# Sigmoid attention and two gated MLPs in float32 parts: GpSimd's share of the weight and operand splitting goes to VectorE and ScalarE, with a new order of loads, identity products ahead of the scores, and other places for some steps

## The chip, the cores and the metric

The kernel runs on one core of a Trainium2 chip. The metric is the device time of one execution in microseconds (us). A core has five engines that run side by side and wait for one another by semaphores: TensorE (PE: products into PSUM), VectorE (DVE), ScalarE (ACT), GpSimd (POOL), and SyncE (SP), which here only issues DMAs. Each engine works off its own list in order.

## The reference

Four batches of 448 rows. Attention has 12 heads of 64, with a sigmoid in place of the softmax; its output, 448 x 768 for each batch, goes through two gated MLPs one after the other, the second with a residual.

```
scores = q k^T / sqrt(64) - log(448);  attn = sigmoid(scores);  x = attn v
MLP 1: h = relu(x w_in);  u, v = halves of h (512 each)
       vn = (v - mean) / sqrt(var + 1e-6)
       x' = (u * (w_spatial vn + b_spatial)) w_out
MLP 2: the same with gelu, vn * g_ln, its own weights, and x' = x + (...) w_out
```

Inputs and weights of the MLPs come as 64-bit floats where the reference has them so (w_in, w_out); the kernel turns them into 32-bit ones itself.

## The kernel before

**Products in parts.** A 32-bit number is split into a high part in a short format (`fp32r`) and the low rest, `lo = x - hi`. A product of two such operands is three products (high x high, high x low, low x high). High parts are written by ScalarE (a cast), low parts by a subtraction.

**Attention** (lines 274 to 445) runs in 12 groups of 4 heads, n = 0 to 11, three to a batch, and each group in 4 rounds, r = 0 to 3, of 128 rows of k (the last has 64). Round s = 4n + r does on TensorE `scores(n, r)` (L357, 24 products of 32 rows side by side into two PSUM tiles `sc`, of which there are three) and `values` of the round two before (L381, into `av`). ScalarE makes the sigmoid of both `sc` tiles (L368). Behind that each round has a step of preparation for the next group: at r = 0 `turn(n+1)` (VectorE transposes k and q, L312 to L317), at r = 1 `high(n+1)` (L325 by VectorE, L328 by ScalarE), at r = 2 `low(n+1)`: two subtractions, that of k by VectorE and that of q by GpSimd (L337). At r = 1 `gather(n-1)` copies the finished `av` of the last group to `x` (L395, VectorE), and only then the next `values` of r = 0 may write there. Loads: `load_qk(n+2)` at r = 1, `load_v(n+2)` at r = 2 (eight small DMAs), `load_v(1)` in round 0.

**The belt.** Weights of the first MLP are made ready meanwhile. `convert` (L152) is a generator for one piece of 128 x 256 64-bit numbers; each `yield` ends what it does in one tick. It loads the piece (L158), squares the upper words (`g`), makes the 32-bit number from the two words by three integer steps on VectorE (L169, L173, L177), sets tiny ones to zero with `g` (L183), casts the high part (L191) and subtracts for the low part (L193). With `early` (27 pieces during attention) GpSimd squares (L164) and subtracts (L193); later ScalarE squares and VectorE subtracts. `belt.tick(new)` lets each running job do one step and starts `new` jobs; in attention it is called once a round, with a new piece in each of rounds 0 to 7 and then in each odd one. `load_w_sp` (spatial weights, four jobs) runs on the belt `spatial` in the last rounds.

**The MLPs** (from L651) take the batches in turn. For each: `hv` (v half, four row blocks, L474), `hu` (u half, L519), `sp` (spatial product, L538, then L544 or L546, L550, and the split of the gated `u` into `gh` by ScalarE, L551, and `gl` by VectorE, L555), `wo` (L572). Between them `fill` ticks three belts; `chain` holds the low-part steps, `gl` among them. `fill(..., waits=True)` ticks `chain` behind the conversions. `store_last` (L605) transposes the last batch by products with `ident` and writes it out by three pairs of DMAs.

Of the kernel before, what the change touches and what calls it, by code (L numbers as in the profile page):

```python
# [9 lines left out]
F32 = mybir.dt.float32  # L10
# [4 lines left out]
ALU = mybir.AluOpType  # L15
# [5 lines left out]
def raw(ap):  # L21
    return ap.bitcast(F32)
# [3 lines left out]
def tile_sigmoid_attention_two_gated_mlps(  # L26
# [125 lines left out]
    def convert(src, n, part, at, keep, early=False):  # L152

        w = stg.tile([P, PIECE, 2], I32, tag="w", name="w", bufs=4)
        dst = w.rearrange("p (c f) two -> p c (f two)", c=n)
        nc.sync.dma_start(out=dst if n > 1 else dst[:, 0], in_=src)  # L158
        yield
        f = stg.tile([P, PIECE], I32, tag="f", name="f", bufs=4)  # L160
        g = stg.tile([P, PIECE], F32, tag="g", name="g", bufs=2)
        low, high = w[:, :, 0], w[:, :, 1]
        if early:
            nc.gpsimd.tensor_tensor(  # L164
                out=g, in0=high.bitcast(F32), in1=high.bitcast(F32), op=ALU.mult
            )
        else:
            nc.scalar.activation(g, high.bitcast(F32), AF.Square)  # L168
        nc.vector.tensor_scalar(  # L169
            out=f, in0=high, scalar1=3, scalar2=0x3FFFFFF8, op0=ALU.logical_shift_left,  # L170
            op1=ALU.bitwise_and,
        )
        nc.vector.scalar_tensor_tensor(  # L173
            out=f.bitcast(U32), in0=low.bitcast(U32), scalar=29, in1=f.bitcast(U32),
            op0=ALU.logical_shift_right, op1=ALU.bitwise_or,
        )
        nc.vector.scalar_tensor_tensor(  # L177
            out=f, in0=high, scalar=-0x40000000, in1=f, op0=ALU.bitwise_and, op1=ALU.bitwise_or
        )
        if early:  # L180
            yield
        f = f.bitcast(F32)
        nc.vector.scalar_tensor_tensor(  # L183
            out=f, in0=g, scalar=TINY * TINY, in1=f, op0=ALU.is_ge, op1=ALU.mult
        )
        yield
        if keep is not None:
            nc.sync.dma_start(out=keep[:, at:at + PIECE], in_=f)
            return
        hi, lo = part()  # L190
        nc.scalar.copy(out=hi, in_=f)  # L191
        yield
        (nc.gpsimd if early else nc.vector).tensor_tensor(  # L193
            out=lo, in0=f, in1=raw(hi), op=ALU.subtract
        )

    def refetch(part, at, n, keep):

# [75 lines left out]
    def attention(apool, epool, ps_att, done):  # L274
# [55 lines left out]
        def low(n):  # L330
# [7 lines left out]

            if n > 0:
                part(nc.vector, 1, slice(0, S))  # L340
                part(nc.gpsimd, 3, slice(0, S))
            else:
                part(nc.vector, 1, slice(0, P))
                part(nc.vector, 3, slice(0, S))
                part(nc.vector, 1, slice(P, S))
# [64 lines left out]
        load_qk(0)  # L410
        load_qk(1)
        load_v(0)
        turn(0)
        high(0)
        low(0)
        for s in range(4 * NG + 2):
# [9 lines left out]
            if n + 1 < NG:  # L426
# [3 lines left out]
                    high(n + 1)  # L430
                elif r == 2:
                    low(n + 1)
            if n + 2 < NG:
                if r == 1:
                    load_qk(n + 2)
                elif r == 2:
                    load_v(n + 2)
            if s == 0:
                load_v(1)
            elif s == 4 * NG - 9:  # L440
                load_vecs(l1)
            belt.tick(1 if s < 8 else s % 2)
            if s >= 4 * NG - 6:
                spatial.tick(1)
        return lambda: gather(NG - 1)

# [1 line left out]
    class Mlp:  # L448
# [111 lines left out]
        def wo(self, b, i, after=None):  # L560
# [8 lines left out]
            for m in range(KD):  # L569
# [7 lines left out]
                for c in done if i == KF - 1 else ():  # L577
                    x = xs[b // 2][:, c, (b % 2) * S:(b % 2 + 1) * S]
                    if L.n == 1:
                        nc.scalar.copy(out=x, in_=self.o[c][:, :S])  # L580
                    else:
                        nc.vector.tensor_tensor(out=x, in0=self.o[c][:, :S], in1=x, op=ALU.add)
                if after and m > 1:
                    after(m - 2)
            if after:
                after(KD - 2)
                after(KD - 1)

    def store(pool, b, m):

# [13 lines left out]

    def store_last(o, pr, m):  # L605

        t = bank()
        for j in range(3, 7):
            nc.tensor.transpose(
# [2 lines left out]
        dst, src = o[:, :, m * P:(m + 1) * P], t.rearrange("p (j f) -> p j f", j=4)  # L612
        if m == KD - 2:
            nc.vector.tensor_copy(out=dst, in_=src)
        else:
            nc.scalar.copy(out=dst, in_=src)
        if m % 2:
            ms = slice((m - 1) * P, (m + 1) * P)
            eng = nc.scalar if m == KD - 1 else nc.sync
            nc.sync.dma_start(  # L620
                out=out[2 * pr + 1, :3 * P, ms].rearrange("(j p) m -> p j m", p=P), in_=o[:, 1:, ms]
            )
            eng.dma_start(out=out[2 * pr + 1, 3 * P:, ms], in_=o[REST:, 0, ms])

    with tc.manual_schedule():
        make_identity(nc, ident)
# [22 lines left out]
        with tc.tile_pool(name="fpool", bufs=1) as fpool:  # L649
# [9 lines left out]
            for n, (m, b) in enumerate(seq):  # L659
# [3 lines left out]
                def fill(new=0, more=(), waits=False):  # L663


                    if refill:
                        belt.waiting += more
                    if not waits:
                        chain.tick()
                    spatial.tick(1)  # L670
                    belt.tick(new)
                    if waits:
                        chain.tick()

                def split_next(c):
                    if nxt:
# [40 lines left out]
                m.sp(b, 1)  # L717
                fill(0 + refill, waits=True)
                m.wo(b, 0)
                fill(1, w_o(0))  # L720
                split_next(2)
                m.sp(b, 2)
                if refill:
                    spatial.waiting = [load_w_sp(l2, j) for j in range(4)]
                fill(0 + refill, waits=True)
                m.wo(b, 1)
                fill(1, w_o(1))
                split_next(4)
                m.sp(b, 3)
                fill(1, waits=True)  # L730
                m.wo(b, 2)
                fill(0 + refill, w_o(2))
                if refill:
# [44 lines left out]
```

## Time and profile before

| | us |
|---|---|
| median of 3 runs | 597.42 (596.37 to 600.14) |
| the profiled execution, its own time | 597.48 |
| its span, first to last instruction | 595.7 |
| busy in the span: TensorE, VectorE, ScalarE, GpSimd | 571.4, 410.0, 251.6, 98.9 |

All times in the trace count from the span's start; 1.8 us of the execution lie outside it. A row of the timeline has start, length, engine, line, operation, tiles and count, and in brackets how long the engine idled before it and what ended that. Lengths of TensorE's rows overlap, since products are pipelined.

### The profile page before, as it was taken

To read this page: it belongs to the slowest core of one execution; us is meant where nothing else is said; L and a number is where in the kernel's file an instruction comes from. 1 tells how busy PE (TensorE), PEld (TensorE's weight loads), DVE (VectorE), ACT (ScalarE), POOL (GpSimd) and SP (SyncE) were. 2 spreads that over 40 slices of the span, in tenths; PEclk is the share of its full clock that TensorE was granted. 3 is DMA by queue.
4 is the path that set the end of the run, shared out by engine and by line. 5 is a ranking of instruction groups with operands and counts; after the bars stand their busy time and mean duration, and the time that the engine had idled before them with its cause. 6 is when DMAs were issued, how large, how long until landed. Compare 5 with 4: busy or idle time off the path is not lost.

```text
span 595.7 us, 9520 instructions
## 1 busy us (share of the span) xinstructions
PE 571.4 (96%) x3568; PEld 456.5 (77%) x3568; DVE 410.0 (69%) x805; ACT 251.6 (42%) x418; POOL 98.9 (17%) x127
## 2 busy tenths in 40 slices
PE   4969999999999999999999999999999999999996
PEld 2535555555469888998888899888989988998995
DVE  4599999999976985894688357669444545544433
ACT  4647877787724434433423345534221313212112
POOL 0445465445221001000200100020010002001000
PEclk9979999999999999999999999999999999999999
DMA  6854446545311212532242224520004100500502
GB/s 185 226 182 136 139 145 196 166 138 119 62 60 35 72 53 72 159 107 62 87 153 80 80 73 114 123 54 18 1 1 77 17 0 12 83 1 0 82 13 92
DMA packets 85405, 51.74 MB, mean 87 GB/s; under 512 B 56112, under 2 KB 75376, under 8 KB 85360
## 3 DMA queue, kind: packets, MB, share of 16 engines
q1 hardware_dynamic: 85280, 51.08, 31.7%
q8 instruction: 28, 0.46, 0.3%
q14 instruction: 17, 0.14, 0.1%
q10 hardware_dynamic: 80, 0.07, 0.0%
HBM read 41.68 MB, written 9.44 MB: 86 GB/s over the span
## 4 chain that ended last, share of the span: by engine, by line
PE 73%; DVE 13%; DMA 4%; issue 3%; ACT 3%; POOL 2%; SPq 1%; DVEq 0%; ACTq 0%
PE t L519 13%; PE t L474 12%; PE sc L572 12%; PE av L381 10%; PE sc L357 10%; PE t L538 10%; PE av L572 6%; DMA w<-in_moe_w_in_dram 2%; DVE f L177 2%; DVE f L173 1%; DMA inq<-in_q_dram 1%; DVE st L483 1%; DVE f L183 1%; POOL st L488 1%; DVE vr L493 1%
## 5 line engine op out<-in xcount | busy, mean ns | idle before, releaser
L368 ACT ACTIVATE a<-sc,small 128x896 f32<-128x896 f32 (+1 forms) x96 | 92.8, 1006 | 32.6 <-PE sc L357 32.3
L357 PEld LDWEIGHTS sc<-ops 32*128 32x128 f32 x1152 | 57.5, 194 | 46.5 <-ACT a L368 25.2
L357 PE MATMUL sc<-ops 32*128 32x448 f32 x1152 | 80.0, 397 | 9.0 <-ACT ops L328 7.5
L519 PE MATMUL t<-xh,uh 128*128 128x448 f32 x192 | 69.9, 364 | 0.9 <-ACT u L523 0.9
L485 POOL TENSOR_SCALAR st<-st 128x1 f32<-128x1 f32 x28 | 10.6, 378 | 356.7 <-DVE st L484 356.7
L381 PE MATMUL av<-a,vt 128*64 128x448 f32 x288 | 64.7, 572 | 5.2 <-DVE x L395 5.0
L519 PE MATMUL t<-xh,ul 128*128 128x448 f32 x192 | 69.5, 362 | 0.0
L519 PE MATMUL t<-xl,uh 128*128 128x448 f32 x192 | 69.3, 361 | 0.0
L474 PE MATMUL t<-vh,xl 128*128 128x512 f32 x168 | 65.7, 391 | 1.3 <-DVE xl L463 1.2
L538 PE MATMUL t<-sh,v 128*128 128x448 f32 x224 | 65.9, 363 | 0.6 <-DVE gt L544 0.6
L474 PE MATMUL t<-vh,xh 128*128 128x512 f32 x168 | 65.6, 390 | 0.0
L474 PE MATMUL t<-vl,xh 128*128 128x512 f32 x168 | 65.4, 389 | 0.0
L551 ACT CAST gh<-u 128x448 fp32r<-128x448 f32 x32 | 18.2, 567 | 103.6 <-DVE u L550 103.6
L483 DVE BATCH_NORM_STATS2 st<-vr 128x6 f32<-128x512 f32 x28 | 19.4, 694 | 53.6 <-ACT vr L480 53.6
L183 DVE SCALAR_TENSOR_TENSOR f<-g,f 128x256 f32<-128x256 f32 x72 | 47.1, 654 | 9.2 <-ACT g L168 3.9
L572 PE MATMUL sc<-gl,oh 128*128 128x448 f32 x128 | 46.7, 365 | 2.1 <-DVE gl L555 2.1
L572 PE MATMUL sc<-gh,oh 128*128 128x448 f32 x128 | 46.5, 363 | 0.0
L572 PE MATMUL sc<-gh,ol 128*128 128x448 f32 x128 | 46.4, 362 | 0.0
L538 PE MATMUL t<-sl,v 128*128 128x448 f32 x128 | 46.3, 362 | 0.0
L538 PEld LDWEIGHTS t<-sh,v 128*128 128x128 f32 x224 | 42.0, 188 | 3.9 <-DVE gt L544 1.2
L381 PEld LDWEIGHTS av<-a,vt 128*64 128x64 f32 x288 | 18.2, 140 | 34.8 <-issue 25.6
L501 ACT CAST v<-vr 128x512 fp32r<-128x512 f32 x24 | 14.9, 621 | 66.0 <-DVE vr L493 66.0
(87 smaller groups left out, 1019.4 us busy)
## 6 DMA issues: line engine op xcount, KB each, us to landing
w<-in_moe_w_in_dram SPq DMA_DIRECT2D x48, 256.0 KB, 3.6
w<-in_moe_w_out_dram SPq DMA_DIRECT2D x24, 256.0 KB, 2.8
ink<-in_k_dram SPq DMA_DIRECT2D x12, 448.0 KB, 4.2
inq<-in_q_dram SPq DMA_DIRECT2D x12, 448.0 KB, 5.1
vt<-in_v_dram SPq DMA_DIRECT2D x48, 96.0 KB, 2.5
out_dram<-y SPq DMA_DIRECT2D x72, 56.0 KB, 1.9
kept<-f SPq DMA_DIRECT2D x30, 128.0 KB, 1.7
w<-kept SPq DMA_DIRECT2D x12, 192.0 KB, 2.6
```

The lines of the kernel that those rows point to most:

```text
L177: nc.vector.scalar_tensor_tensor(out=f, in0=high, scalar=-0x40000000, in1=f, op0=ALU.bitwise_and, op1=ALU.bitwise_or)
L183: nc.vector.scalar_tensor_tensor(out=f, in0=g, scalar=TINY * TINY, in1=f, op0=ALU.is_ge, op1=ALU.mult)
L357: nc.tensor.matmul(sc[h // 2][:, h % 2, :S], w[ps, o:o + P], ops[n][ps, y, S * j:S * (j + 1)], start=(t == 0), stop=(t == 5), tile_positio ...
L368: nc.scalar.activation(a[:, 2 * x:2 * x + 2] if r < 3 else a[ps], sc[x][ps, :, :S], AF.Sigmoid, bias=bias_s[ps], scale=scale,)
L381: nc.tensor.matmul(avp[n][x][o * D:(o + 1) * D, :S], vt[:, h, r] if r < 3 else vr[ps, o], a[:, h] if r < 3 else a[ps, o], start=(r == 0), ...
L474: nc.tensor.matmul(ps[:, :FF], a, w[:, c, :], start=(c == 0 and n == 0), stop=(c == KD - 1 and n == 2),)
L483: nc.vector.bn_stats(out=st, in_=vr)
L501: nc.scalar.copy(out=pair[0], in_=vr)
L519: nc.tensor.matmul(ps[:, :S], w, a, start=(c == 0 and n == 0), stop=(c == KD - 1 and n == 2))
L538: nc.tensor.matmul(ps[:, :S], a, w, start=(n == 0), stop=(n == len(todo) - 1))
L551: nc.scalar.copy(out=gh, in_=u)
L572: nc.tensor.matmul(self.o[m][:, :S], w, a, start=(i == 0 and n == 0), stop=(i == KF - 1 and n == 2),)
```

## The change

GpSimd no longer takes part in attention: the low part of q, the pieces' squares and the pieces' subtractions go to VectorE (`low`, L192) and ScalarE (square). With `early` a piece waits one tick more between its load and its first step. The first piece is loaded ahead of round 0, none is started in rounds 3 and 7; `load_v(n+1)` is called behind `load_qk(n+2)` at r = 1. 18 products of `ident` with itself are put ahead of round 0. `load_w_sp` and `load_vecs` start two rounds earlier. In the MLPs `gl` (a step of `chain`) runs between the second and third integer step of the first piece converted in that `fill`, where there is one; three pieces are started in later batches instead of batch 0 (`rate`). In the last stage the transposes come one tile later, the last tile is copied by two engines and tiles 4 and 5 are written out apart.

```diff
@@ convert
         yield
+        if early:
+            yield
...
-        if early:
-            nc.gpsimd.tensor_tensor(
-                out=g, in0=high.bitcast(F32), in1=high.bitcast(F32), op=ALU.mult
-            )
-        else:
-            nc.scalar.activation(g, high.bitcast(F32), AF.Square)
+        nc.scalar.activation(g, high.bitcast(F32), AF.Square)
...
+        if not early:
+            later.pop("between", lambda: None)()
...
-        (nc.gpsimd if early else nc.vector).tensor_tensor(
-            out=lo, in0=f, in1=raw(hi), op=ALU.subtract
-        )
+        nc.vector.tensor_tensor(out=lo, in0=f, in1=raw(hi), op=ALU.subtract)
@@ low
-                part(nc.gpsimd, 3, slice(0, S))
+                part(nc.vector, 3, slice(0, S))
@@ attention
         load_v(0)
+        belt.tick(1)
+
+        warm = ps_att.tile([P, 2, 512], F32, tag="sc", name="sc")
+        for _ in range(18):
+            nc.tensor.matmul(warm[:, 0, :P], ident, ident, start=True, stop=True)
         turn(0)
...
-            if n + 2 < NG:
-                if r == 1:
+            if r == 1:
+                if n + 2 < NG:
                     load_qk(n + 2)
-                elif r == 2:
-                    load_v(n + 2)
-            if s == 0:
-                load_v(1)
-            elif s == 4 * NG - 9:
+                if n + 1 < NG:
+                    load_v(n + 1)
+            if s == 4 * NG - 11:
                 load_vecs(l1)
-            belt.tick(1 if s < 8 else s % 2)
-            if s >= 4 * NG - 6:
+            belt.tick(s % 2 if s > 7 else s not in (3, 7))
+            if s >= 4 * NG - 8:
                 spatial.tick(1)
@@ wo
+                    h = S - 2 * P if after and c == KD - 1 else 0
+                    for ts in ((slice(0, h), slice(h, S)) if h else (slice(0, S),)):
...
-                if after and m > 1:
-                    after(m - 2)
+                if after and m > 2:
+                    after(m - 3)
@@ store_last
-            nc.scalar.copy(out=dst, in_=src)
-        if m % 2:
-            ms = slice((m - 1) * P, (m + 1) * P)
+            nc.scalar.copy(out=dst[:, :2], in_=src[:, :2])
+            nc.vector.tensor_copy(out=dst[:, 2:], in_=src[:, 2:])
+        if m % 2 or m == KD - 2:
+            ms = slice((m if m > 3 else m - 1) * P, (m + 1) * P)
             eng = nc.scalar if m == KD - 1 else nc.sync
+            eng.dma_start(out=out[2 * pr + 1, 3 * P:, ms], in_=o[REST:, 0, ms])
...
@@ fill
-                    if not waits:
+                    if waits:
+                        later["between"] = chain.tick
+                    else:
                         chain.tick()
                     spatial.tick(1)
                     belt.tick(new)
-                    if waits:
-                        chain.tick()
+                    later.pop("between", lambda: None)()
+
+                rate = 0 if n == 0 else 1
@@ the three calls behind wo(0), wo(1) and sp(3)
-                fill(1, w_o(0))
+                fill(rate, w_o(0))
```

Three places show how the lists of the engines move. The first is SyncE's list at the start of attention, behind the first loads of k, q and `vt_100` (v of group 0); `w_...` are pieces, `ink`/`inq` k and q of group 2, and `vt`/`vr` with another number v of a later group. Before, from the end of `load_v(0)` on:

```order
L302 DMA vr_101<-in_v_dram 32x2x64
L297 DMA vt_158<-in_v_dram 32x4x192
L302 DMA vr_159<-in_v_dram 32x2x64
...
L158 DMA w_168<-in_moe_w_in_dram 128x512
L285 DMA ink_201<-in_k_dram 128x896
L285 DMA inq_203<-in_q_dram 128x896
L158 DMA w_211<-in_moe_w_in_dram 128x512
```

And now, from the same DMA on:

```order
L299 DMA vr_101<-in_v_dram 32x2x64
L158 DMA w_110<-in_moe_w_in_dram 128x512
L158 DMA w_179<-in_moe_w_in_dram 128x512
L282 DMA ink_212<-in_k_dram 128x896
L282 DMA inq_214<-in_q_dram 128x896
L294 DMA vt_216<-in_v_dram 32x4x192
L299 DMA vr_217<-in_v_dram 32x2x64
```

The first two pieces have moved ahead of the eight DMAs of the second v (six of them left out above) and of k and q of group 2.

The second place is ScalarE's list in the middle of attention, rounds r = 0 to 3 of group 3; the activations are the sigmoids, two to a round, the cast of `tq` is `high`, those to `vh` are high parts of pieces, `g` is a square. Before:

```order
L368 ACTIVATE a_732<-sc_707,small_70 128x896
L191 CAST vh1_302<-f_663 128x256
L368 ACTIVATE a_779<-sc_753,small_70 128x896
L368 ACTIVATE a_779<-sc_754,small_70 128x896
L328 CAST ops_745<-tq_740 128x896
L368 ACTIVATE a_824<-sc_798,small_70 128x896
L368 ACTIVATE a_824<-sc_799,small_70 128x896
L191 CAST vh1_302<-f_747 128x256
```

And now the like rounds of a group:

```order
L365 ACTIVATE a_911<-sc_886,small_70 128x896
L365 ACTIVATE a_953<-sc_927,small_70 128x896
L365 ACTIVATE a_953<-sc_928,small_70 128x896
L325 CAST ops_924<-tq_919 128x896
L190 CAST vh1_313<-f_877 128x256
L165 ACTIVATE g_986<-w_883 128x256
L365 ACTIVATE a_1019<-sc_993,small_70 128x896
L365 ACTIVATE a_1019<-sc_994,small_70 128x896
```

The casts of pieces have moved from the even rounds to the odd ones, and the squares have joined them there.

The third place is VectorE's list behind the first `sp` of batch 0, from the gating to `gl`; `f` is a piece in the making. Before:

```order
L550 TENSOR_TENSOR u_2607<-gt_2720,u_2607 128x448
L193 TENSOR_TENSOR ol12_2696<-f_2656,oh12_2695 128x256
L193 TENSOR_TENSOR ol12_2696<-f_2663,oh12_2695 128x256
L169 TENSOR_SCALAR f_2729<-w_2706 128x256
L173 SCALAR_TENSOR_TENSOR f_2729<-w_2706,f_2729 128x256
L177 SCALAR_TENSOR_TENSOR f_2729<-w_2706,f_2729 128x256
L183 SCALAR_TENSOR_TENSOR f_2729<-g_2730,f_2729 128x256
L555 TENSOR_TENSOR gl_2722<-u_2607,gh_2721 128x448
```

And now:

```order
L550 TENSOR_TENSOR u_2626<-gt_2739,u_2626 128x448
L192 TENSOR_TENSOR ol12_2715<-f_2675,oh12_2714 128x256
L192 TENSOR_TENSOR ol12_2715<-f_2682,oh12_2714 128x256
L166 TENSOR_SCALAR f_2748<-w_2725 128x256
L170 SCALAR_TENSOR_TENSOR f_2748<-w_2725,f_2748 128x256
L555 TENSOR_TENSOR gl_2741<-u_2626,gh_2740 128x448
L176 SCALAR_TENSOR_TENSOR f_2748<-w_2725,f_2748 128x256
L182 SCALAR_TENSOR_TENSOR f_2748<-g_2749,f_2748 128x256
```

`gl` stands two steps of a piece further ahead.

## Rows read from the trace of the kernel before

**Rows 1.** The page, its part on busy time (us, share of the span, instructions).

```profile
PE 571.4 (96%) x3568; PEld 456.5 (77%) x3568; DVE 410.0 (69%) x805; ACT 251.6 (42%) x418; POOL 98.9 (17%) x127
```

**Rows 2.** Windows: us busy of PE, PEld, DVE, ACT, POOL; granted clock, DMA share, GB/s.

```profile
36.00:39.00 3.00, 3.00 (x12) 0.66 (x12) 2.93 (x7) 0.41 (x1) 1.48 (x2) 0.50 0.89 279
...
60.00:80.00 20.00, 20.00 (x218) 10.73 (x220) 19.59 (x32) 15.20 (x20) 10.85 (x9) 1.00 0.49 143
```

**Rows 3.** Timeline, start of attention (start, us, engine, line, operation, tiles, count).

```profile
1.00 0.29 POOL masks.py:199 TENSOR_SCALAR_AFFINE_SELECT ident<-ident 128x128 f32<-128x128 f32 x1
...
7.53 1.09 DVE L337 TENSOR_TENSOR ops<-tq,ops 128x896 fp32r<-128x896 f32 x1 [0.57 <-ACT ops L328]
...
7.55 3.36 PE L357 MATMUL sc<-ops 32*128 32x448 f32 x26 [7.55 <-ACT ops L328]
...
9.39 1.04 DVE L312 STREAM_TRANSPOSE tk<-ink 128x384 f32<-128x384 f32 x2
...
11.54 0.58 DVE L325 CAST ops<-tk 128x896 fp32r<-128x896 f32 x1
...
11.64 2.61 PE L357 MATMUL sc<-ops 32*128 32x448 f32 x24 [0.73 <-ACT a L368]
...
13.96 0.43 SPq L158 DMA_DIRECT2D w<-in_moe_w_in_dram  x1
...
18.38 0.29 DVE L169 TENSOR_SCALAR f<-w 128x256 int32<-128x256 int32 x1 [6.25 <-DMA w<-in_moe_w_in_dram]
```

**Rows 4.** Timeline around the stop of round 6.

```profile
32.31 2.16 POOL L337 TENSOR_TENSOR ops<-tq,ops 128x896 fp32r<-128x896 f32 x1
...
32.57 2.18 DVE L177 SCALAR_TENSOR_TENSOR f<-w,f 128x256 int32<-128x256 int32 x1
...
35.63 3.25 PE L381 MATMUL av<-a,vt 128*64 128x448 f32 x8 [5.01 <-DVE x L395]
...
47.99 1.79 PE L357 MATMUL sc<-ops 32*128 32x448 f32 x24
```

**Rows 5.** Groups by line, VectorE, 0 to 165 us (xcount, busy us, mean ns, idle before).

```profile
L183 DVE SCALAR_TENSOR_TENSOR f<-g,f 128x256 f32<-128x256 f32 x27 | 27.9, 1034 | 1.1
...
L177 DVE SCALAR_TENSOR_TENSOR f<-w,f 128x256 int32<-128x256 int32 x27 | 17.5, 649 | 0.9
...
L337 DVE TENSOR_TENSOR ops<-tk,ops 128x896 fp32r<-128x896 f32 x11 | 15.3, 1393 | 0.0
```

**Rows 6.** Groups by line, VectorE, 165 to 420 us.

```profile
L183 DVE SCALAR_TENSOR_TENSOR f<-g,f 128x256 f32<-128x256 f32 x45 | 19.1, 425 | 8.0 <-ACT g L168 3.9
```

**Rows 7.** Timeline, rounds 13 to 15, ScalarE and the scores.

```profile
59.12 1.91 ACT L368 ACTIVATE a<-sc,small 128x896 f32<-128x896 f32 x2 [0.88 <-PE sc L357]
...
59.88 1.79 PE L357 MATMUL sc<-ops 32*128 32x448 f32 x24
...
60.91 0.94 ACT L328 CAST ops<-tq 128x896 fp32r<-128x896 f32 x1
...
61.74 1.92 ACT L368 ACTIVATE a<-sc,small 128x896 f32<-128x896 f32 x2
...
63.24 1.50 PE L357 MATMUL sc<-ops 32*128 32x448 f32 x24
```

**Rows 8.** Timeline, two squares in a row, and eight transposes of the end.

```profile
188.87 0.75 ACT L168 ACTIVATE g<-w 128x256 f32<-128x256 f32 x2
...
588.92 1.04 PE L609 MATMUL t<-ident,x 128*128 128x128 f32 x8
```

**Rows 9.** Groups by line, ScalarE, the table load in the MLPs.

```profile
L480 ACT ACT_TABLE_LOAD x1 | 1.3, 1283 | 0.0
```

**Rows 10.** Timeline, hand-over to the MLPs.

```profile
166.21 0.50 PE L474 MATMUL t<-vh,xl 128*128 128x512 f32 x1 [1.17 <-DVE xl L463]
```

**Rows 11.** Timeline, first and last of three waits for gl.

```profile
203.46 0.47 PE L572 MATMUL sc<-gl,oh 128*128 128x448 f32 x1 [0.84 <-DVE gl L555]
...
309.27 0.47 PE L572 MATMUL sc<-gl,oh 128*128 128x448 f32 x1 [0.58 <-DVE gl L555]
```

More of the change, by code (lines that the diff above doesn't have):

```diff
@@ L580, in wo @@
                         nc.scalar.copy(out=x, in_=self.o[c][:, :S])
-                    else:
-                        nc.vector.tensor_tensor(out=x, in0=self.o[c][:, :S], in1=x, op=ALU.add)
-                if after and m > 1:
-                    after(m - 2)
+                        continue
+                    h = S - 2 * P if after and c == KD - 1 else 0
+                    for ts in ((slice(0, h), slice(h, S)) if h else (slice(0, S),)):
+                        nc.vector.tensor_tensor(
+                            out=x[:, ts], in0=self.o[c][:, ts], in1=x[:, ts], op=ALU.add
+                        )
+                if after and m > 2:
+                    after(m - 3)
             if after:
-                after(KD - 2)
-                after(KD - 1)
+                for m in range(KD - 3, KD):
+                    after(m)
     def store(pool, b, m):
@@ L614, in store_last @@
             nc.vector.tensor_copy(out=dst, in_=src)
-        else:
-            nc.scalar.copy(out=dst, in_=src)
-        if m % 2:
-            ms = slice((m - 1) * P, (m + 1) * P)
+        elif m < KD - 2:
+            nc.scalar.copy(out=dst, in_=src)
+        else:
+            nc.scalar.copy(out=dst[:, :2], in_=src[:, :2])
+            nc.vector.tensor_copy(out=dst[:, 2:], in_=src[:, 2:])
+        if m % 2 or m == KD - 2:
+            ms = slice((m if m > 3 else m - 1) * P, (m + 1) * P)
             eng = nc.scalar if m == KD - 1 else nc.sync
+            eng.dma_start(out=out[2 * pr + 1, 3 * P:, ms], in_=o[REST:, 0, ms])
             nc.sync.dma_start(
@@ L622, in store_last @@
             )
-            eng.dma_start(out=out[2 * pr + 1, 3 * P:, ms], in_=o[REST:, 0, ms])
     with tc.manual_schedule():
@@ L726, in tile_sigmoid_attention_two_gated_mlps @@
                 m.wo(b, 1)
-                fill(1, w_o(1))
+                fill(rate, w_o(1))
                 split_next(4)
                 m.sp(b, 3)
-                fill(1, waits=True)
+                fill(rate, waits=True)
                 m.wo(b, 2)
```

## Prediction

> **What bounds the kernel now.** I began with the page's busy shares: TensorE works in 96% of the span [rows 1], so a change gains only where TensorE waits or runs at its lower clock, and about 24 us of the span are open. The windows and the timeline put most of that into the first 48 us. The products start at 7.55, when the first operands are split; 24 score products then take 2.61 us where the same 24 take 1.50 later [rows 3, 7], so the clock is at its lower level there, although no clock row shows it that early. At 34 us comes the largest hole: the `av` products of round 6 start at 35.63 after 5.01 us of waiting for VectorE's gather (L395), and behind the hole the granted clock is 0.50, the lower level [rows 2, 4]: eight records take 3.25 us.
>
> Why is VectorE late? Two reasons stand in rows. It idles 6.25 us until 18.38 for the first weight piece, whose load SyncE issues at 13.96, behind both loads of v [rows 3]. Then its own work is stretched beside GpSimd: at 32.57 the step L177 takes 2.18 us, next to GpSimd's 2.16 us of L337 [rows 4]. Over attention L183 averages 1034 ns and L177 649; L183, of the same shape, averages 425 once GpSimd is nearly idle [rows 5, 6].
>
> From round 10 on (47.99) a group of four rounds takes 11.88 us: 47.99 to 59.88, the same round one group on [rows 4, 7]. There TensorE is full (20.00 of 20) and VectorE too (19.59) [rows 2]. Behind attention TensorE waits 1.17 us at the hand-over, and three times, first 0.84 and last 0.58 us, for `gl` (L555) [rows 10, 11].
>
> **The start.** The identity products need `ident`, ready at 1.29 (1.00 + 0.29), and must be over when scores can start at 7.55. The nearest row is the transposes of the last stage, 128 columns too: eight records in 1.04 us at the higher level, 0.13 each [rows 3, 8]. A plain fp32 product leaves two records (the four `av` products leave eight [rows 4]), so 18 give 36 records: 4.7 us at the higher level, twice that at the lower, an end between 6.1 and 10.8. I take the middle, about 8: the scores lose nothing by it, since their second third waits for the low part of q anyway, 7.53 + 1.09 = 8.62 [rows 3]. The late end costs 10.8 - 8.6 = 2.2 us at most. If the products bring the clock up, round 0 ends at 8.65 + two thirds of 1.50 = 9.65. Each next round waits for the first activation of the one before, 1.0 us (half of 1.91 and its end [rows 7]): round 1 goes on at 10.8 and ends at 12.2, round 2 goes on at 13.3. From there eight rounds at the steady pace lead to round 10 at 13.3 + 2 x 11.88 = 37.1, against 47.99: **10.9 us gained**, if no stall takes the place of the one at 35.63.
>
> Would one? SyncE now issues the first piece where the second load of v began, eight DMAs earlier by the order. Eight issues take 8 x 0.43 us or a little more (the length of one, [rows 3]), so it goes out near 10.4, and with the 4.4 us it needed before (13.96 to 18.38) it is there by 14.8; I take 13.5, as less is in flight then. VectorE's queue from there, with at most 4 x 0.425 = 1.7 us for a piece's four steps [rows 6], 1.09 for half a low(n) and 2.15 for a turn(n) (9.39 to 11.54, [rows 3]): three steps of piece 0 to 14.8, low(1) to 17.0, pieces 1 and 2 to 20.4, turn(2) to 22.5, a step and a subtraction, three steps of piece 3: 24.7. The gather of group 0 can start when round 5's `av` products end: round 2 goes on at 13.3, three rounds of 3.1 follow, then round 5's scores (1.50) and its half-height `av` (half of 1.6): 24.9. So it is on time, with little to spare; the loads of group 2 and v(1) are queued behind w0 and w1, and are wanted only from 19 on. Group 1's gather comes out 0.6 us late, for VectorE has 6 pieces in the first 8 rounds: a stall of about 0.4. Net **10.5**, between 6 (late products and a gather 2 us late) and 10.9.
>
> **Steady rounds, VectorE.** It takes over the low part of q (1.09, [rows 3]) and two weight subtractions (at most 0.43 each, by L183's width) per group: +1.95. It is rid of GpSimd: 0.61 + 0.22 us for each of two pieces, 0.30 at L337 [rows 5, 6], so at least -1.96. 11.64 us of 11.88 (98%) remain as they are at worst. TensorE is full here in spite of VectorE's 98%, so I count nothing either way; if VectorE runs over, by the two subtractions at their upper bound, it costs 0.2 us a group, 1.6 in all.
>
> **Steady rounds, ScalarE.** This is where the change costs. By the order, round r = 1 of a group now has cast, copy and square between the activations, where the cast stood alone. Before: activations at 59.12, cast 60.91, next activation 61.74, its first half done about 62.75, scores of the round after from 63.24, whose third product is the first that needs it: 0.55 us of slack [rows 7]. The square takes 0.32 in a row (two in 0.75), the copy hardly differs: 0.65 together [rows 8]. With 0.1 for the signal the slack is overrun by 0.2 us, in 8 groups: **-1.6**. At the full 0.43 each it is 0.4 a group, -3.2; if the copy hides in its neighbours, 0.
>
> **The rule on tables.** The program loads a table for Sigmoid at its start and one for Gelu later, which takes 1283 ns [rows 9], and no other, although Square already runs beside Relu and Gelu, and the order of the change still prints two. The Trainium skill, page "ScalarE: Activation LUTs", section "Table sets: the hidden batching unit", says that functions come in sets, that a switch of set costs a load (about 2.7 us with its drain), and its list names no Square in Sigmoid's set. By that rule the squares between the sigmoids would cost two loads for each of 27 pieces; by the order they cost none, and the sum takes none.
>
> **The hand-over and the MLPs.** `load_w_sp` starts two rounds earlier and VectorE's backlog at round 46 grows: the last gather comes about a microsecond late, -0.8 (0 to -1.2). In return the `xl` subtractions no longer wait behind it, and the 1.17 us of [rows 10] go. But batch 0 is VectorE's queue: what TensorE gains it waits for at the next `gl`. There three subtractions of GpSimd's come back (0.4 each) while `gl` leaves two steps earlier (2 x 0.425). I book +0.75 for the hand-over (1.17 less one subtraction) and +0.85 for the order: **+1.6** (0.5 to 3.5). In batch 2 the wait of 0.58 [rows 11] is shorter than those 0.85 us, and vanishes: **+0.8** with the refill behind it (0 to 1.2). Three pieces move from batch 0 to batch 2; VectorE has 30% idle time there [page share 69%, rows 1], so nothing for them, 0.5 if one meets a `gl`.
>
> **The end.** The last DMA is now half as large, but SyncE has one more to issue before it (0.43, [rows 3]). The one hides the other: nothing, +-0.5.
>
> **The sum**, against the profiled execution's 597.48 us (span 595.7; the median of the three runs is 597.42): 10.5 - 1.6 - 0.8 + 1.6 + 0.8 = 10.5, so **587.0 us**.
>
> **The rivals.**
> *The clock stays low at the start.* The products come, but rounds 0 to 2 run as now, each 2.61 - 1.50 = 1.1 us longer [rows 3, 7]: 590.3. For it: between rounds 0, 1 and 2 TensorE still pauses a microsecond each. Against: at 1 us TensorE has never worked before, and the products fill just that. 0.12.
> *VectorE is late all the same.* A piece that lands 3 us later puts the gather of group 0 behind the scores; TensorE stops, and the clock falls as it did at 36. The hole costs some 2.5 us and the lower clock behind it about as much: 592. For it: my queue has half a microsecond to spare. 0.10.
> *ScalarE becomes the pacer (the slower side).* The copy waits for VectorE's L182 and stands ahead of the next sigmoids; before, that wait existed too, but with no square behind it, and in even rounds. If VectorE is over 2 us behind in each of the 20 odd rounds with a piece, each loses 1.5 - 0.55 = 0.95 us: 19 us, so 606. It decides from 0.55 us of waiting per round. Against: GpSimd's stretch is gone. 0.05.
> *Square reloads the tables.* 54 loads of 1.28 us, 69 in all: 656. The order prints none: 0.01.
> *The forecast*, 587.0, 582.5 to 590 by its bounds (all terms at their better ends give 581.4, which hardly meet, so 582.5; the start and the ScalarE term half way to their worse ones give 590): 0.72.
>
> **How the numbers follow.** The predicted time is that of the forecast. From 582.5 to 591.5 lie the forecast, the low clock and a part of the late VectorE: 0.82 to 0.85 of the chance. A measurement of this kernel can tell about 1% from no change: faster means under 591.4, which holds for the forecast and the low clock (0.84) less what spills over; the late VectorE is the same; only ScalarE as the pacer and the tables are slower. So 0.82, 0.13, 0.05.
>
> **What would show it.** Right: scores at about 7.6 with 24 products in 1.50 us; no hole near 35 us and no clock row under 1.00 behind 10 us; L183 at 0.43 us throughout; round 10 at 37; groups of 12.1 us; TensorE's waits for L555 gone in batch 2. Wrong: groups of 12.5 us or more with TensorE waiting for activations (ScalarE was undervalued); an `av` product that waits microseconds for the gather (VectorE's queue was); products that end behind 9 us.

## The result, and the profile after

| | before | after |
|---|---|---|
| median of three runs, us | 597.42 (596.37 to 600.14) | 591.45 (589.38 to 592.36) |
| ratio after / before, 95% interval | | 0.9898 [0.9869, 0.9927] |
| span of the profiled execution | 595.7 | 589.7 |

The change makes the kernel 1.0% faster (0.7 to 1.3). The forecast was 587.0. The median lies inside the stated range, 582.5 to 591.5, by 0.05 us only, and that is luck: the three runs lie 3 us apart, and the forecast's own bounds, 582.5 to 590, do not hold it. The mechanisms mostly came as forecast, but the start gave 6.7 us where 10.5 were booked, so most of this section is about the start.

The page's busy line of the changed kernel, to be held against [rows 1]: VectorE has less to do although it took over GpSimd's work.

```profile
PE 574.2 (97%) x3604; PEld 461.6 (78%) x3604; DVE 391.1 (66%) x845; ACT 261.4 (44%) x445; POOL 27.3 (5%) x62
```

The windows of [rows 2], in the changed kernel (us, then busy us of PE, PEld, DVE, ACT, POOL, granted clock, DMA share, GB/s). The clock is at its upper level between 36 and 39, where it was 0.50, and VectorE, with 19.59 of 20 us before, has four free.

```profile
36.00:39.00 3.00, 3.00 (x36) 1.50 (x36) 2.93 (x10) 2.40 (x4) 0.00 (x0) 1.00 0.89 186
60.00:80.00 20.00, 20.00 (x222) 10.83 (x220) 15.76 (x42) 16.10 (x24) 0.00 (x0) 1.00 0.57 176
```

Groups by line, VectorE, 0 to 160 us (count, busy us, mean ns): L182 is the step that was L183 and took 1034 ns on average beside GpSimd [rows 5]; it now has the length of [rows 6].

```profile
L182 DVE SCALAR_TENSOR_TENSOR f<-g,f 128x256 f32<-128x256 f32 x25 | 10.4, 416 | 0.1
L166 DVE TENSOR_SCALAR f<-w 128x256 int32<-128x256 int32 x26 | 7.5, 287 | 7.1 <-DMA w<-in_moe_w_in_dram 7.1
```

The timeline of the start (start, us, engine, line, operation, tiles, count, idle before and its end), which answers to [rows 3, 4]:

```profile
1.34 6.12 PE L414 MATMUL sc<-ident 128*128 128x128 f32 x36 [1.34 <-POOL ident masks.py:199]
...
7.46 0.68 PE L354 MATMUL sc<-ops 32*128 32x448 f32 x8
...
10.77 1.49 PE L354 MATMUL sc<-ops 32*128 32x448 f32 x24 [0.91 <-ACT a L365]
10.91 0.36 SPq L282 DMA_DIRECT2D ink<-in_k_dram  x1
11.37 0.38 SPq L282 DMA_DIRECT2D inq<-in_q_dram  x1
...
17.67 0.31 SPq L294 DMA_DIRECT2D vt<-in_v_dram  x1
...
19.59 0.31 SPq L299 DMA_DIRECT2D vr<-in_v_dram  x1
...
19.97 1.96 SPq L158 DMA_DIRECT2D w<-in_moe_w_in_dram  x3
...
24.32 0.29 DVE L166 TENSOR_SCALAR f<-w 128x256 int32<-128x256 int32 x1 [5.93 <-DMA w<-in_moe_w_in_dram]
24.39 0.43 ACT L165 ACTIVATE g<-w 128x256 f32<-128x256 f32 x1 [4.13 <-DMA w<-in_moe_w_in_dram]
...
25.91 2.61 PE L354 MATMUL sc<-ops 32*128 32x448 f32 x22 [3.00 <-ACT a L365]
...
41.28 1.74 PE L354 MATMUL sc<-ops 32*128 32x448 f32 x24
```

The identity products end as the scores begin, and round 1 runs 24 products in 1.49 us instead of 2.61. Then a new stall: ScalarE stands 4.13 us at the square of the third piece (L165), whose load has not landed; round 4's sigmoids stand behind it on the same engine; TensorE waits 3.00 us for them, and the 22 products after that take 2.61 us, the length that 24 have at the lower clock level (the granted clock is 0.50 from 25.9 to 28.5). The load is late because SyncE issues it only at 19.97. Between it and the second piece stand k and q of group 2 and the eight loads of v(1), and the last two of these are held at 17.67 and 19.59. The waits of SyncE's queue (0 to 40 us) say for what: the DMAs of k and q, each eight places ahead of the one held.

```profile
SPq L294 <- DMA ink<-in_k_dram: 6.6, 4, 2.6
SPq L299 <- DMA inq<-in_q_dram: 6.5, 5, 2.1
```

Round 10 starts at 41.28 instead of 47.99 (37.1 was forecast). In the steady part, the rows of the timeline that answer to [rows 7]: in round r = 1 cast, copy and square stand ahead of the sigmoids, which start at 55.63, and 24 products of r = 3 take 1.68 us. A group takes 12.06 to 12.10 us (seven in a row, by the half-height `av` products from 52.21 to 136.77) instead of 11.88.

```profile
54.16 0.94 ACT L325 CAST ops<-tq 128x896 fp32r<-128x896 f32 x1
...
54.99 0.42 ACT L190 CAST vh<-f 128x256 fp32r<-128x256 f32 x1
...
55.29 0.45 ACT L165 ACTIVATE g<-w 128x256 f32<-128x256 f32 x1
...
55.63 1.91 ACT L365 ACTIVATE a<-sc,small 128x896 f32<-128x896 f32 x2
...
56.50 1.68 PE L354 MATMUL sc<-ops 32*128 32x448 f32 x24
```

What TensorE waits for in the whole span (engine, tile, line, released by; us in total, times, longest). The waits for `xl`, the low part of `x` [rows 10], are gone, and those for `gl` [rows 11] are down from 2.1 to 0.7 us. But those for `gt`, which VectorE makes of the spatial product (L544, L546), have grown from 0.6 to 2.4. Two lines of before, and those of the changed kernel:

```profile
PE sc L572 <- DVE gl L555: 2.1, 3, 0.8
PE t L538 <- DVE gt L544: 0.6, 1, 0.6
```

```profile
PE sc L354 <- ACT a L365: 4.8, 3, 3.0
...
PE t L538 <- DVE gt L544: 1.2, 2, 1.0
PE t L538 <- DVE gt L546: 1.2, 1, 1.2
PE sc L572 <- DVE gl L555: 0.7, 2, 0.5
```

Where the time went, by how much earlier the same product starts than before (the refill is the first MLP's batch 3, in which the weights of the second MLP are brought in):

| stretch | ahead at its end, us | gained in it | booked |
|---|---|---|---|
| start, to round 10 | 6.71 (47.99, 41.28) | +6.7 | +10.5 |
| groups to the last scores, with the gather at round 46 | 5.17 (158.81, 153.64) | -1.5 | -1.6 and -0.8 |
| hand-over, first `hv` block and batch 0 | 7.56 (219.56, 212.00) | +2.4 | +1.6 |
| batch 1 | 6.72 (277.12, 270.40) | -0.8 | 0 |
| batch 2 | 7.45 (324.69, 317.24) | +0.7 | +0.8, with the refill |
| batch 3 and the refill, to the first `wo` of the second MLP | 6.93 (414.77, 407.84) | -0.5 | in the row above |
| second MLP, to its last `wo` | 6.31 (580.03, 573.72) | -0.6 | 0 |
| the end | 6.0 (595.7, 589.7) | -0.3 | 0 |

### The profile page after: what moved, and what is told of

Read it like the earlier page. It is cut to its first block, busy times and chain, and to the rows that moved or that the text cites. A ratio compares the mean times of both kernels' runs of the same rounds, so it can differ in the third digit from the quotient of the medians.

```text
span 589.7 us, 9543 instructions
## 1 busy us (share of the span) xinstructions
PE 574.2 (97%) x3604; PEld 461.6 (78%) x3604; DVE 391.1 (66%) x845; ACT 261.4 (44%) x445; POOL 27.3 (5%) x62
## 4 chain that ended last, share of the span: by engine, by line
PE 71%; DVE 13%; DMA 6%; ACT 4%; issue 2%; POOL 2%; SPq 1%; DVEq 0%; ACTq 0%
PE t L474 13%; PE sc L572 11%; PE sc L354 11%; PE av L378 11%; PE t L519 10%; PE t L538 9%; PE av L572 6%; DMA w<-in_moe_w_in_dram 3%; DVE f L170 2%; DVE st L483 1%; DVE f L182 1%; DVE f L176 1%; DMA vt<-in_v_dram 1%; POOL st L488 1%; DVE vr L493 1%
## 5 line engine op out<-in xcount | busy, mean ns | idle before, releaser
L354 PE MATMUL sc<-ops 32*128 32x448 f32 x1152 | 78.7, 385 | 5.4 <-ACT a L365 4.8
L378 PE MATMUL av<-a,vt 128*64 128x448 f32 x288 | 62.0, 552 | 0.0
L165 ACT ACTIVATE g<-w 128x256 f32<-128x256 f32 x72 | 31.0, 438 | 18.1 <-DMA w<-in_moe_w_in_dram 13.7
L519 PEld LDWEIGHTS t<-xh,uh 128*128 128x128 f32 x192 | 36.0, 188 | 2.8 <-ACT u L523 0.4
```

Of the source, the lines that this page charges most:

```text
L354: nc.tensor.matmul(sc[h // 2][:, h % 2, :S], w[ps, o:o + P], ops[n][ps, y, S * j:S * (j + 1)], start=(t == 0), stop=(t == 5), tile_positio ...
L378: nc.tensor.matmul(avp[n][x][o * D:(o + 1) * D, :S], vt[:, h, r] if r < 3 else vr[ps, o], a[:, h] if r < 3 else a[ps, o], start=(r == 0), ...
L519: nc.tensor.matmul(ps[:, :S], w, a, start=(c == 0 and n == 0), stop=(c == KD - 1 and n == 2))
```

## The experiments

Theory: the loss at the start is an order of loads. The third piece stands behind v(1) in SyncE's queue, and its square carries the wait to the sigmoids. Rivals: VectorE's own queue; the bandwidth of the loads; the clock. Each kernel below also ran beside the kernel before, whose medians were 596.8 to 598.1.

**Pieces ahead of v** (the kernel with early pieces, below). Only the place of the issues on SyncE changes:

```diff
+            if s in (1, 2):
+                belt.tick(1)
             if r == 1:
                 if n + 2 < NG:
                     load_qk(n + 2)
-                if n + 1 < NG:
+                if 0 < n < NG - 1:
                     load_v(n + 1)
+            if s == 2:
+                load_v(1)
...
-            belt.tick(s % 2 if s > 7 else s not in (3, 7))
+            if s not in (1, 2):
+                belt.tick(s % 2 if s > 7 else s not in (3, 7))
```

> The changed kernel, but the third and fourth weight piece are issued on SyncE ahead of the loads of q and k of group 2 and of v of group 1. Theory (load order): the third piece landed at 24.3 us because SyncE held its issue until 19.97 behind eight loads of v; its square on ScalarE kept round 4's sigmoids waiting 4.13 us, and 3.8 us of the start's gain went there. Then the wait of the square goes, the 22 score products of round 4 run without a wait of 3.00, round 10 starts near 37.4 instead of 41.28, and the time is 587.6 (591.45 - 3.8), 587.0 to 588.3. Rival (bandwidth): the pieces only push the transfers of q and k behind them later; VectorE then waits for k at its transpose, the gather of group 0 comes late, and 590 to 591.5 is measured. Rival (VectorE's own work is too long for these rounds): the pieces are there but the av products wait 2 us or more for the gather: 589.5.

587.31 us (586.21 to 588.11), ratio 0.9823 [0.9801, 0.9845]: 4.1 us below the changed kernel, as the theory has it. SyncE's and ScalarE's rows of its timeline, and the scores:

```profile
10.81 1.38 SPq L158 DMA_DIRECT2D w<-in_moe_w_in_dram  x3
...
13.34 2.52 PE L354 MATMUL sc<-ops 32*128 32x448 f32 x22 [0.92 <-ACT a L365]
...
21.87 0.43 ACT L165 ACTIVATE g<-w 128x256 f32<-128x256 f32 x1
...
22.57 1.91 ACT L365 ACTIVATE a<-sc,small 128x896 f32<-128x896 f32 x2 [0.27 <-PE sc L354]
...
24.12 1.50 PE L354 MATMUL sc<-ops 32*128 32x448 f32 x24
```

ScalarE does not idle ahead of the third square (21.87), where it stood 4.13 us, and the sigmoids follow TensorE. The bandwidth rival falls, and so does VectorE's: no av product waits for the gather. One thing the expectation did not have: in this execution, the slowest of the five, the clock fell in round 2 (22 products 2.52 us behind a pause of 0.92), so round 10 starts at 38.31. In the kernel with the same loads further below (`gl` behind the pieces) it did not (1.51 us), and round 10 starts at 36.50, against my 37.1.

**Squares of the first pieces on VectorE.** The loads stay late; only the carrier changes.

```diff
-        nc.scalar.activation(g, high.bitcast(F32), AF.Square)
+        if early and len(belt.waiting) > l1.late - 6:
+            nc.vector.tensor_tensor(
+                out=g, in0=high.bitcast(F32), in1=high.bitcast(F32), op=ALU.mult
+            )
+        else:
+            nc.scalar.activation(g, high.bitcast(F32), AF.Square)
```

> The changed kernel, but the squares of the first pieces are made by VectorE (a product of the piece with itself) instead of ScalarE; the loads stay in their order. Theory A (the late load holds both engines): ScalarE no longer waits for the third piece and round 4's sigmoids come on time, but VectorE stands until 24.3 us as before, with the transposes of group 2 and the gather of group 0 behind it: the av products of round 6 wait for the gather until about 29, so that of the 3.8 us at most 1.5 come back: 590 to 591.5, and a wait of av for x (L392) of 2 us or more is in the trace. Theory B (the square on ScalarE is the only carrier): round 10 starts near 37.5 and the time is 587.6 to 588.3.

591.77 us (589.50 to 593.11): theory A, 0.3 above its range. Its timeline shows VectorE waiting for the piece, and TensorE then for the gather, behind VectorE's backlog:

```profile
22.70 0.43 DVE L166 TENSOR_TENSOR g<-w 128x256 f32<-128x256 f32 x1 [4.27 <-DMA w<-in_moe_w_in_dram]
...
29.37 1.75 PE L383 MATMUL av<-a,vt 128*64 128x448 f32 x8 [2.62 <-DVE x L397]
```

In this execution, the fastest of the four, round 10 starts at 39.56; theory B had it near 37.5. So ScalarE is where the wait hit first, but the cause is the load: both engines that touch a piece have work behind it that TensorE needs.

**Without the identity products**, on the changed kernel and on the one with early pieces (`range(18)` becomes `range(1)`).

> The changed kernel with one identity product in place of 18, so TensorE has hardly worked when the scores start. Theory: rounds 0 to 2 run at the lower clock, 24 products in 2.61 instead of 1.50 us, but round 4 waits for the third weight piece until 24.39 whatever TensorE did before, so the products are worth nearly nothing here: 591.4 to 592.2, with the wait of the score products for the activation shorter than 3.00 by what the rounds before it took longer. Rival: the products' worth is what rounds 0 to 2 lose, three times 1.1 us, wherever the load lands: 594.7.

> The kernel with the third and fourth piece issued earlier, and one identity product in place of 18. Theory: with the load's stall gone the identity products are worth what they save in rounds 0 to 2: three times 1.1 us, so this is 3.0 us (2.5 to 3.5) above the kernel that has the same loads and 18 products, about 590.6, and the same 24 products take 2.61 us in rounds 0 to 2 and 1.50 from round 3 or 4 on. Rival: even so another load or VectorE's queue holds round 4 or 5, and the difference is under 1 us.

590.50 us (590.11 to 590.93) and 590.13 (589.59 to 590.44). In the changed kernel the products gain nothing: the time without them is 0.9 below the 591.45 with them. That is under the range of the theory, but inside the 3 us by which the changed kernel's own runs differ. With early pieces they are worth 2.8 us (587.31 with them), as the theory has it. The first one's timeline shows why: rounds 0 to 2 run slowly, and what they lose comes off the wait for the piece.

```profile
11.64 2.61 PE L354 MATMUL sc<-ops 32*128 32x448 f32 x24 [0.73 <-ACT a L365]
...
24.92 0.44 ACT L165 ACTIVATE g<-w 128x256 f32<-128x256 f32 x1 [1.20 <-DMA w<-in_moe_w_in_dram]
...
25.91 2.02 PE L354 MATMUL sc<-ops 32*128 32x448 f32 x24
```

**The kernel before with the identity products alone** (18 products ahead of `turn(0)`).

> The kernel before, with nothing changed but 18 identity products ahead of the first scores. Theory: in the kernel before, the start is set by VectorE, which waits for the first weight piece until 18.4 us and is then stretched beside GpSimd; rounds 0 to 2 end 3 us earlier, but the av products of round 6 wait for the gather until 35.6 as before, so the time stays at 597 (596.3 to 597.6), with a wait of 7 to 8 us for x (L395) instead of 5.01. Rival: what the products save in rounds 0 to 2 stays saved: 593.8.

597.57 us (596.26 to 600.84, ten runs), ratio 1.0015 [0.9994, 1.0036]: nothing. The scores of round 2 end 2.7 us earlier (14.90 instead of 17.59), and the stop of round 6 ends within 0.01 us of where it did in [rows 4] (35.63):

```profile
11.01 1.50 PE L357 MATMUL sc<-ops 32*128 32x448 f32 x24 [0.90 <-ACT a L368]
...
35.64 3.25 PE L381 MATMUL av<-a,vt 128*64 128x448 f32 x8 [7.51 <-DVE x L395]
```

**GpSimd's part alone undone**, with early pieces: squares, weight subtractions and the low part of q on GpSimd again.

> The kernel with the two pieces issued earlier (587.3 us), but GpSimd again makes the squares, the weight subtractions and the low part of q in attention. Theory: from round 10 on ScalarE has no squares, so groups take 11.88 instead of 12.08, 1.6 us less; at the start VectorE's steps on a piece are stretched (L182 and L176 well over 0.43 us) and the gather of group 0 or 1 comes late by up to 2 us. Together 585.7 to 588.5. Rival: taking GpSimd out was what made the start fast: VectorE is late by 4 us or more, the av products of round 6 wait for the gather, the clock falls behind it, 591 or more.

589.74 us (589.26 to 590.48), 2.4 above the same kernel without GpSimd; neither number of mine. Groups take 11.89 to 11.97 us, as expected, and the gather of group 0 is on time. But TensorE waits 1.51 us for that of group 1, and stands 2.07 us in round 46 while the gather of group 10 starts only at 148.40 (the profile names no releaser there); this second stall I had not priced. Its groups by line (VectorE, 0 to 160 us) and its timeline:

```profile
L171 DVE TENSOR_SCALAR f<-w 128x256 int32<-128x256 int32 x26 | 24.1, 926 | 0.8 <-DMA w<-in_moe_w_in_dram 0.8
L187 DVE SCALAR_TENSOR_TENSOR f<-g,f 128x256 f32<-128x256 f32 x25 | 14.7, 587 | 0.2
```

```profile
40.00 1.76 PE L385 MATMUL av<-a,vt 128*64 128x448 f32 x8 [1.51 <-DVE x L399]
...
148.40 1.91 DVE L399 COPY x<-av 128x378 f32<-128x378 f32 x8
...
149.52 1.91 PE L385 MATMUL av<-a,vt 128*64 128x448 f32 x8 [2.07 <-issue]
```

The step that takes 287 ns in the changed kernel (L166) takes 926 beside GpSimd (L171). What GpSimd's removal brings is slack on VectorE at both ends of attention, not in the middle.

**Copies in even rounds**, with early pieces:

```diff
         hi, lo = part()
+        if early:
+            yield
         nc.scalar.copy(out=hi, in_=f)
```

> The kernel with the two pieces issued earlier (587.3 us), and one more step between VectorE's last step on a piece and ScalarE's copy of it, so that copies fall into even rounds and squares stay in odd ones. Theory: a group takes 12.08 us instead of 11.88 because in round r = 1 cast, copy and square stand between the sigmoids; with the copy gone from there a group takes 11.88 again, the scores of r = 3 run 24 products in 1.50 instead of 1.73, and the time falls by 8 x 0.2 = 1.6 us to 585.7 (585.2 to 586.3). Rival: the 0.2 us come from VectorE, which took over work from GpSimd and is late with something in each group; then groups stay at 12.08 and the time at 587.3.

586.27 us (584.74 to 587.67). The groups take 11.88 to 11.89 us, seven in a row, with VectorE doing all that it does in the changed kernel: the 0.2 us a group are ScalarE's, and the rival falls. Its timeline in the same round r = 1 as above: the sigmoids follow the square, and 24 products of r = 3 take 1.50 us.

```profile
49.79 0.93 ACT L327 CAST ops<-tq 128x896 fp32r<-128x896 f32 x1
...
50.62 0.45 ACT L165 ACTIVATE g<-w 128x256 f32<-128x256 f32 x1
...
50.97 1.90 ACT L367 ACTIVATE a<-sc,small 128x896 f32<-128x896 f32 x2
...
52.12 1.50 PE L356 MATMUL sc<-ops 32*128 32x448 f32 x24
```

The median fell by 1.0 us only, with runs 3 us apart; the next experiment is on those.

**Identity products between rounds 0, 1 and 2**, on top of it (the fillers; `busy(n)` issues n identity products into a bank of the av pool):

```diff
+        busy(20)
...
             if s > 1:
                 values(*divmod(s - 2, 4))
+            else:
+                busy(3)
```

> The kernel with the two pieces issued earlier and the copies in even rounds (586.27 us, its runs 584.74 to 587.67), with 20 identity products ahead of the scores and three more behind the scores of round 0 and of round 1, where TensorE stood for 0.9 us each until the first activation was done. Theory: the runs of that kernel differ by up to 3 us because in some of them the clock falls in one of these pauses (in the profile of the kernel with early pieces the 22 products of round 2 took 2.52 us, in that with copies in even rounds 1.48); with the pauses filled every run starts at the higher level, the median falls to the lowest run of before, 585.0 (584.5 to 585.7), and the runs lie within 1.5 us. Rival: the spread has another cause (the landing of the first loads); then median and spread stay at about 586.2 and 3 us.

585.72 us, six runs from 585.17 to 586.06. The spread went from 2.9 to 0.9 us as the theory has it; the median fell by 0.55 where 1.3 were expected. The fillers themselves cost nothing: from the first scores to round 10 the profile takes 29.15 us with them (7.64 to 36.79) and 29.13 without (7.79 to 36.92, in the fastest run, 584.74). It falls behind that run only in the refill, by 0.9 us between 394 and 400, where a wait for `u` is new. Nor is the clock the only cause of the spread: a run of the last kernel below, which has no fillers, took 588.22 us at a mean granted clock of 0.999.

**`gl` behind the pieces' steps again**, with early pieces (`chain.tick` behind `belt.tick`):

> The kernel with the two pieces issued earlier (587.3 us), but the subtraction for gl stands behind the steps on the pieces again, as it did before, and not between them. Theory: TensorE's waits for L555 (gl) come back, three times 0.6 to 0.8 us in batches 0 and 2; against 0.5 us of them now: +1.5, 588.8 (588 to 590). Rival: what is won at gl is waited for at gt two products later on the same queue of VectorE, and the time stays at 587.3 with fewer waits for gt.

588.82 us (588.37 to 592.04), 1.5 above: the theory. TensorE's waits:

```profile
PE sc L577 <- DVE gl L560: 2.6, 3, 1.2
...
PE t L543 <- DVE gt L551: 1.1, 1, 1.1
PE t L543 <- DVE gt L549: 1.0, 1, 1.0
```

Three waits for `gl` are back; those for `gt` are as long as without this edit, so the one is not traded for the other.

**Three pieces more in batch 0**, on the kernel with fillers (`rate = 1` throughout):

> The kernel with early pieces, copies in even rounds and identity products between the first rounds (585.72 us), but batch 0 of the MLPs starts three pieces more, as it did before the change. Theory: the new wait of 1.1 us for gt (L546) at about 400 us, in the refill, comes from the three pieces that were moved to later batches and still stand on VectorE's queue there; with them back in batch 0 it goes, while waits for gl (L555) of 0.5 to 1 us come back in batch 0: 585.0 to 586.3, and the wait for L546 is gone from the trace. Rival: the wait for L546 has nothing to do with the moved pieces: it stays at 1.1 us, and the waits in batch 0 come on top: 586.3 to 587.

585.37 us (584.81 to 586.07), ratio 0.9786 [0.977, 0.9803], the fastest kernel of all. The wait for `gt` at the refill (L546 in the changed kernel, L559 in the kernel with fillers), 1.1 us there, is gone, and no wait came back in batch 0:

```profile
PE t L551 <- DVE gt L557: 1.1, 1, 1.1
PE t L532 <- ACT u L536: 0.7, 2, 0.4
PE sc L585 <- DVE gl L568: 0.5, 1, 0.5
```

The median moved by 0.35 only, and waits for `u`, which ScalarE writes, grew from 0.5 to 0.7 us; where the wait for `gt` came from is settled by the trace, the medians alone would not do it. This execution also loses 1.0 us in attention, which the edit does not touch: VectorE stands for a spatial weight, the gather of group 10 (L394) starts behind that, at 145.99, and the `av` products of round 46 wait (the profile names no releaser), with no work of GpSimd's beside them:

```profile
144.90 0.65 DVE L225 STREAM_TRANSPOSE tsp<-wsp 128x448 f32<-128x448 f32 x1 [1.00 <-DMA wsp<-in_moe_w_spatial_dram]
...
147.10 1.91 PE L380 MATMUL av<-a,vt 128*64 128x448 f32 x8 [1.14 <-issue]
```

**One issue less ahead of the last store**, on the kernel with copies in even rounds:

> The kernel of the experiment with copies in even rounds, and at the very end the 64 last rows of the last two column blocks go out in one transfer issued by ScalarE, so that SyncE has one issue less ahead of the last store. Theory: in the changed kernel the last store was ready at 585.1 and was issued behind another at about 585.9; without that the span ends 0.5 us earlier behind TensorE's last product (5.45 us behind it before this edit, 4.9 then), and the time is 0.5 below that experiment: about 585.2. Rival: the last transfer is bound by its landing or by the larger transfer on ScalarE's queue, and nothing is gained.

586.23 us (585.42 to 588.22) against 586.27: nothing. The span ends 5.5 us behind TensorE's last product with and without the edit. SyncE's last issue is out 1.83 us behind that product instead of 2.22, and the end does not follow, so the count of issues is not what sets it. What does was not tried.

## Why the prediction was right, and where not

**Start, the step that failed.** Up to round 3 all came as written: identity products over by 7.5 (8 was taken), rounds 1 and 2 on at 10.77 and 13.18 (10.8 and 13.3). The failing sentence is "the loads of group 2 and v(1) are queued behind w0 and w1, and are wanted only from 19 on". They are, but the third piece is queued behind them, and it is wanted at 20.3, when ScalarE comes to its square (24.39 - 4.13). I drew up VectorE's queue as if pieces were always there and left SyncE's out behind the second; and I costed the squares by their length, not by what they wait for. Of the signs written down, round 10 at 37 and no clock row under 1.00 behind 10 us did not come, and the stall is none of the three signs of being wrong. The rival "VectorE is late all the same" named a late piece, a fallen clock and 592, and all three came; but the piece came 5.93 us after VectorE was free for it, not 3, and the wait that TensorE met came by ScalarE, one round before VectorE's own backlog would have made it (the experiment with squares on VectorE shows that one).

**Identity products.** "The clock comes up" held; their worth did not. They gain 3 us of products only if nothing later waits for a load: 0 in the kernel before and in the changed one, 2.8 with early pieces. The rival "the clock stays low" is out in the profiled execution of the changed kernel, though with 0.9 us pauses left the clock falls in some executions.

**Steady rounds.** VectorE at nothing: right, 11.88 us a group with all of GpSimd's work on it. I counted on at least 1.96 us a group of relief from GpSimd. Over seven whole groups VectorE is busy 9.87 us a group (69.07 us from 52.21 to 136.77) instead of 11.57 (80.96 us from 58.96 to 142.16): 1.70 freed in spite of the added 1.95, so the relief is 3.65, nearly twice what I counted on. ScalarE at -0.2 us a group: right in size (12.08 against 11.88) and in cause (copies moved away). The rival of ScalarE as the pacer did not come: VectorE is not behind.

**Tables.** The trace has two table loads in the whole program, as before, of 1283 ns each [rows 9], with 26 squares between sigmoids. The rule of the Trainium skill, page "ScalarE: Activation LUTs", section "Table sets: the hidden batching unit", as I applied it to Square, which its list of Sigmoid's set does not name but leaves open, does not agree with that.

**Hand-over.** The gather at round 46 was booked at -0.8 and cost nothing (the same scores start at 153.64 with no wait ahead of them): I priced the earlier `load_w_sp` on a VectorE still stretched by GpSimd, and the experiment with GpSimd back shows that stall, 2.07 us. But the experiment with three pieces more shows 1.14 us at the same products without GpSimd, when a spatial weight lands late, so that it cost nothing in the changed kernel's profile was partly luck. The hand-over itself gave 1.8, as the `xl` subtractions are early enough; with batch 0 2.4 instead of 1.6.

**MLPs.** Batch 2 and the refill behind it, booked at +0.8 together, gave +0.7 and -0.5. "Three pieces move from batch 0 to batch 2 ... so nothing for them" failed: they come due in the refill, where VectorE has no idle time ahead of `gt`, and cost 1.3 us there; 1.0 of it had just been won, as two waits for `u` that the refill had before are gone. Batch 1 lost 0.8, half of it at a wait for `gl` (the product at 253.32 starts 0.46 us later than the spacing of its neighbours); why VectorE is later there was not tested. In the second MLP 0.6 us went in steps of 0.01, most of them in `sp` and `wo`, with no wait; left open. The end was booked at 0 +-0.5 and is -0.3. Behind the start the terms missed by +1.7 and -2.3 us, which nearly cancel: that the whole falls short by little more than the start's 3.8 us is luck too.

## What to carry to other kernels

Draw up the issuing engine's queue like any other: for each load that moves, list what now stands ahead of it until it is out, and which engine meets its first consumer. A gain ahead of a wait that ends with a DMA is worth nothing until that DMA moves: find the last such wait of a stage first. An instruction that waits for a load does not belong on an engine whose next instruction TensorE needs at once. Here moving it to another engine gained nothing, since TensorE needs that one too, and issuing the load earlier gained 4.1 us; giving the instruction one round more than the change does was not tried.

## What the runs showed of the hardware

- Beside a working GpSimd, VectorE's three integer steps and the product of a piece took 587 to 926 ns on average (the kernel with GpSimd's part undone), without it 287 to 425 (the changed kernel). In the kernel before, a GpSimd that is busy half of the time (41.21 us from 58.96 to 142.16) cost VectorE 1.70 us in each group of 11.88 more than the work that it took away.
- The clock in the first rounds differs from execution to execution: in two kernels that are the same up to the MLPs (early pieces, and `gl` behind the pieces) 22 products took 2.52 us behind a pause of 0.92 us and 1.51 behind one of 0.91. With identity products in these pauses, on the kernel with copies in even rounds, the runs moved from 2.9 to 0.9 us apart.
- In SyncE's queue a DMA was held until the one eight places ahead had landed: k, issued at 10.91, let go the load of v at 17.67, and q, issued at 11.37, that at 19.59.
